# Issuing one head pair's values and the next pair's scores as one step of the attention that runs beside the feed-forward

## The chip, the cores and the metric

One core of one Trainium2 chip runs the whole kernel. The metric is device time in microseconds (us). A kernel is run several times and the median is given; one further execution was recorded by the hardware profiler, and all views shown here come from it.

## The reference

Four batches of 768 tokens go through two blocks, all in float32. The first is attention with 8 heads of 64: each token sees the tokens nearer than 16 places and 24 block summaries (maximum of the keys, mean of the values, over blocks of 32 tokens). The second takes the heads side by side as x of 768 x 512, adds the real part of a two-dimensional Fourier transform, normalises, and adds a feed-forward with 2048 hidden units.

```python
k_sum = k.reshape(B, H, nb, block, D).max(axis=3)
v_sum = v.reshape(B, H, nb, block, D).mean(axis=3)
scores_l = scale * q @ k.T                  # masked to |i - j| < 16
scores_s = scale * q @ k_sum.T + log(32)
a = softmax(concat([scores_l, scores_s]))   # over both together
x = a @ concat([v, v_sum])                  # heads side by side: (4, 768, 512)
u = x + real(fft(fft(x, axis=1), axis=2))
un = (u - mean(u)) / sqrt(var(u) + 1e-6)
out = u + relu(un @ w_ch1) @ w_ch2          # 512 -> 2048 -> 512
```

## The kernel before

The instructions are written in Python as generators. A scheduler puts them into each engine's queue by program order as priority, moving an instruction that it expects to be ready ahead of one that it does not; once written, each queue runs in that order.

**Stages.** The attention of batch 0 comes first, in an order fixed by hand (`first_attention`). Then, for each batch b: the Fourier stage and normalisation (`gen_fourier`, lines 1043 to 1160), and the feed-forward in two halves, `gen_hidden(b, 0)`, `gen_out(b, 0)`, `gen_hidden(b, 1)`, `gen_out(b, 1)`. Products use a seven-product scheme for 2 x 2 blocks, so `gen_hidden` has four j of seven products each and yields four times per j: 16 steps; `gen_out` of a first half has 12 steps. The chain `most` of hidden, out, hidden is thus 44 steps. The second out half runs together with the next batch's Fourier stage. During batch 0 the weights are also converted from 64-bit to 32-bit floats (`gen_weights`), by VectorE (DVE) and ScalarE (ACT), and stored for the later batches.

**Attention of batches 1 to 3.** `gen_attention(b)` (line 884) runs beside the previous batch's stages. A batch has four head pairs g. For each pair:

- `prepare` (line 676): 12 transposes on TensorE (PE) into four PSUM tiles `qk`, eight ACT copies into `kt` and `qt` (line 698), and a DVE maximum over the key blocks, `km` (line 700). It is issued one pair ahead.
- `scores` (line 751): 48 small matrix products of the near keys into two PSUM tiles `sc` (line 759), an exponential on ACT for each (line 765) and a DVE multiplication of each by the mask `near`.
- `sum_scores` (line 769): four products with the block maxima into the tile `ss` (line 775) and an exponential on ACT (line 776).
- `values` (line 778): one product for the block means into the PSUM tile `vs` (line 782), a DVE multiplication into the SBUF tile of the same name, 48 small products into two PSUM tiles `av` (line 792), six more that add the block means (line 797), then for each `av` a DVE reciprocal (line 801) and a DVE multiplication into x.

The profile counts two PE records for each of these products. `load` and `load_values` issue the DMAs of q, k and v for later pairs on the SP queue, on which the feed-forward's weights are fetched too.

**PSUM.** The eight banks are two pools of four: `abank` (tag `attn`) for every attention tile above and for the Fourier stage of later batches, `bank` for the feed-forward (tiles X, Y, Z).

**A hidden j in four steps.** Step 1: product into X, ACT copies X to c11 (line 1187); product into Y, DVE adds it. Step 2: product into X, ACT copies X to c12 (line 1192); product into Z, ACT copies it to c22 (line 1194). Step 3: product into X, DVE adds X to c22; product into Z, DVE adds. Step 4: product into X, ACT writes c21 (line 1203); the rest is DVE. X accumulates over four products, so each product into X waits until the reading of the one before has ended.

**Mixing.** `drive` takes its generators in proportion. Counting the steps of `most`, the 12 attention steps of a batch come after

```
scores                  4  15  26  37
sum_scores + prepare    8  19  30  41
values + load_values   11  22  33  44
```

for the attention of batches 2 and 3. For batch 1 six steps fall into the Fourier stage of batch 0 (the first of them a prepare of its own), and the other seven go one to four steps of `most`, beside twelve steps of weights.

Of the kernel before, what the change touches and what calls it, by code (L numbers as in the profile page):

```python
# [489 lines left out]
def _main_program(ctx, tc, q, k, v, moe_w_ch1, moe_w_ch2, out):  # L490
# [3 lines left out]
    B, H, S, D = q.shape  # L494
# [5 lines left out]
    NP = H // 2  # L500
# [54 lines left out]
    def abank(shape, name):  # L555
        return psum.tile(shape, FP, tag="attn", bufs=4, name=name)
# [6 lines left out]
    def tt(out, in0, in1, op):  # L563
        nc.vector.tensor_tensor(out=out, in0=in0, in1=in1, op=op)  # L564
# [7 lines left out]
    def load(b, g, *which):  # L572

        for n in which or (1, 0):
            t = nat[b, g, n] = apool.tile([P, 2, NST // 2, 2 * D], FP, tag="nat", bufs=4, name=f"{'qk'[n]}n_{b}_{g}")
            fetch(out=t.rearrange("p e j n -> p (e j) n"),
                  in_=(q, k)[n][b, 2 * g:2 * g + 2].rearrange("e (j p s) d -> p (e j) (s d)", p=P, s=2))
# [61 lines left out]
    def load_values(b, g):  # L639
        if is_wide(b):  # L640
            load_wide_values(b, g)
            return
        if g % 2 and following(b, g, 1) and (b, g) != (1, 1):
            block_sums(*divmod((b * NP + g + 1) // 2, NP // 2))
        load_narrow_values(b, g)

    def load_wide_values(b, g):

        vw, off = wide_vw(g), v[b, 2 * g].offset
        for r0, r1, i0, i1 in ((0, WK, 1, NQ - 1), (W, WK, 0, 1), (0, WK - W, NQ - 1, NQ)):  # L650
            for e in range(2):
                fetch(out=vw[r0:r1, e, i0:i1, 0:D],
                      in_=bass.AP(v.tensor, off + (S * e + QB * i0 - W + r0) * D,
                                  [[D, r1 - r0], [QB * D, i1 - i0], [1, D]]))
# [96 lines left out]
    def scores(b, g):  # L751
        kt, qt = kt_bufs[g % 2], nat[b, g]
        ps = [abank([P, NB2, BLOCK], f"sc_{b}_{g}_{h}") for h in range(2)]
        for i in range(NB2):
            for h in range(2):
                o = BLOCK * (NB2 * h + i)
                for e in range(2):
                    rows, r = slice(D * e, D * (e + 1)), 64 * (e ^ h)
                    nc.tensor.matmul(ps[h][r:r + 64, i, :], kt[rows, o:o + 64], qt[rows, o:o + BLOCK],  # L759
                                     start=True, stop=True)  # L760
        p = apool.tile([P, 2, NQ, QB], FP, tag="p", name=f"p_{b}_{g}")
        pm = p[:, 1].rearrange("p n c -> p (n c)")[:, 0:S2]
        p = p[:, 0].rearrange("p (h i) (j c) -> p h (i j) c", h=2, c=BLOCK)
        for h in range(2):
            nc.scalar.activation(out=p[:, h], in_=ps[h], func=AF.Exp, scale=SC)
            tt(p[:, h], p[:, h], near[:, h], ALU.mult)
        return p, pm

    def sum_scores(b, g, p):
        km, qt = km_bufs[g % 2], nat[b, g]  # L770
        ps = abank([P, S2], f"ss_{b}_{g}")
        for h in range(2):
            for e in range(2):
                rows, r = slice(D * e, D * (e + 1)), 64 * (e ^ h) + 32 * h
                nc.tensor.matmul(ps[r:r + 32, :], km[rows, :], qt[rows, S2 * h:S2 * (h + 1)], start=True, stop=True)
        nc.scalar.activation(out=p, in_=ps, func=AF.Exp, scale=SC)

    def values(b, g, p, pm, x):
        vw = vw_bufs[g % 2]
        ps = abank([P, D], f"vs_{b}_{g}")  # L780
        vb, pick = sums[b, g]
        nc.tensor.matmul(ps, pick, vb, start=True, stop=True)
        tt(vs[:, :, 0:D], ps[:, None, :].to_broadcast([P, 2, D]),
           half_of[:, :, None].to_broadcast([P, 2, D]), ALU.mult)

        av = [abank([P, NST, D1], f"av_{b}_{g}_{r}") for r in range(2)]
        for t in range(NST):
            h = t // HT
            for j in range(4):
                for r in range(2):  # L790
                    rows, i = slice(64 * r, 64 * (r + 1)), 4 * t + j
                    nc.tensor.matmul(av[r][32 * j:32 * (j + 1), t, :], p[rows, h, i - NB2 * h, :], vw[rows, i, :],
                                     start=(t == 0), stop=False, skip_group_check=True)
        for t in range(HT):
            for r in range(2):
                rows = slice(64 * r, 64 * (r + 1))
                nc.tensor.matmul(av[r][:, t:t + HT + 1:HT, :], pm[rows, P * t:P * (t + 1)], vs[rows],
                                 start=False, stop=(t == HT - 1), skip_group_check=True)
        for r in range(2):
            rc = rec[:, b * NP + g, r]  # L800
            nc.vector.reciprocal(out=rc, in_=av[r][:, :, D])
            xo = x[:, 0, P * g + D * r:P * g + D * (r + 1)]
            xo = bass.AP(xo.tensor, xo.offset, [list(xo.ap[0]), [HT * DM + D * (1 - 2 * r), 2], [DM, HT], [1, D]])
            tt(xo, av[r].rearrange("p (h t) d -> p h t d", h=2)[:, :, :, 0:D],
               rc.rearrange("p (h t) -> p h t", h=2)[:, :, :, None].to_broadcast([P, 2, HT, D]), ALU.mult)
# [3 lines left out]
    def following(b, g, n):  # L809
        i = b * NP + g + n  # L810
        return divmod(i, NP) if i < B * NP else None
# [72 lines left out]
    def gen_attention(b):  # L884
        x = bpool.tile([P, NST, DM], FP, tag="x", bufs=2, name=f"x_{b}")
        x_of[b] = x
        for g in range(NP):
            p, pm = scores(b, g)
            yield
            sum_scores(b, g, pm)  # L890
            n1, n2, n3 = (following(b, g, n) for n in (1, 2, 3))
            if n1:
                prepare(*n1)
            if n3:
                load(*n3)
            yield
            values(b, g, p, pm, x)
            if n2:
                load_values(*n2)
            yield  # L900


# [402 lines left out]
    def drive(*gens):  # L1305


        gens = list(gens)
        rounds = max(g[1] for g in gens)
        while gens:  # L1310
            for s in range(rounds):
                for g in list(gens):
                    gen, n, ahead = g
                    for _ in range(n * (s + 1) // rounds - n * s // rounds):
                        with tc.high_priority(ahead) if ahead else ExitStack():
                            done = next(gen, gens) is gens
                        if done:
                            gens.remove(g)
                            break

    def first(gen, n):
        for _, step in zip(range(n), gen):
            yield

    weights = gen_weights()
# [15 lines left out]
        yield from gen_attention(1)  # L1341

    attn = second_attention()
    drive((gen_fourier(0), 4, 600), (first(weights, 66), 12, 0), (first(attn, 6), 1, 0))
    block_sums(1, 1)
    for b in range(B):


        most = chain(gen_hidden(b, 0), gen_out(b, 0), gen_hidden(b, 1))
        if b == 0:  # L1350
            in_order[0] = False
            drive((most, 4, 0), (weights, 12, 0), (attn, 1, 0))
            done_weights.append(True)
        else:
            drive((most, 11, 0), (gen_attention(b + 1) if b + 1 < B else iter(()), 3, 0))
        last = gen_out(b, 1)
        if b + 1 < B:
            drive((gen_fourier(b + 1), 22, 600), (last, 12, 0))
        else:
            drive((last, 1, 0))  # L1360
        if b == B - 2:

            ok = apool.tile([P, B * NP * 2 * NST], FP, tag="qt", name="ok")
            all_ok = spool.tile([P, 2], FP, tag="all_ok", name="all_ok")
            flag = cpool.tile([1, 1], I32, name="flag")
            rv = rec.rearrange("p n h i -> p (n h i)")
            nc.vector.tensor_scalar(out=ok, in0=rv, scalar1=1.0 / LIM, scalar2=None, op0=ALU.is_ge)
            nc.vector.scalar_tensor_tensor(out=ok, in0=rv, scalar=LIM, in1=ok, op0=ALU.is_le, op1=ALU.mult)
            nc.vector.tensor_reduce(out=all_ok[:, 0:1], in_=ok, op=ALU.min, axis=AX.X)
            nc.vector.memset(all_ok[:, 1:2], 1.0)  # L1370
            ps = bank([1, 1], "flag_ps")
            nc.tensor.matmul(ps, all_ok[:, 0:1], all_ok[:, 1:2], start=True, stop=True)
            nc.vector.tensor_scalar(out=flag, in0=ps, scalar1=P - 0.5, scalar2=None, op0=ALU.is_lt)
# [40 lines left out]
```

## Time and profile before

| | |
|---|---|
| median of 3 runs | 826.65 us (822.34 to 828.26) |
| the profiled execution | 829.18 us, of which 827.4 us is the span of the instructions |
| PE, share of the span | 97% |
| DVE, ACT, POOL | 59%, 31%, 2% |
| DMA | 120.53 MB, mean 146 GB/s |

Busy time is how long an engine had an instruction in it; for PE the ends of matrix products are modelled and overlap, so the starts are the better measure. In a timeline row the columns are the start and the length in us, the engine, the line, the operation with the tile it writes and those it reads, their shapes, and how many instructions are merged in the row; a bracket gives idle time of the engine before it and what ended that. "PEld" is the loading of PE's stationary operand.

### The profile page before, as it was taken

To read this page: it belongs to the slowest core of one execution; us is meant where nothing else is said; L and a number is where in the kernel's file an instruction comes from. 1 tells how busy PE (TensorE), PEld (TensorE's weight loads), DVE (VectorE), ACT (ScalarE), POOL (GpSimd) and SP (SyncE) were. 2 spreads that over 40 slices of the span, in tenths; PEclk is the share of its full clock that TensorE was granted. 3 is DMA by queue.
4 is the path that set the end of the run, shared out by engine and by line. 5 is a ranking of instruction groups with operands and counts; after the bars stand their busy time and mean duration, and the time that the engine had idled before them with its cause. 6 is when DMAs were issued, how large, how long until landed. Compare 5 with 4: busy or idle time off the path is not lost.

```text
span 827.4 us, 14641 instructions
## 1 busy us (share of the span) xinstructions
PE 798.8 (97%) x6038; PEld 583.6 (71%) x6038; DVE 486.9 (59%) x1117; ACT 254.6 (31%) x561; POOL 20.0 (2%) x31
## 2 busy tenths in 40 slices
PE   9979998999999999999999999999999999999997
PEld 6767655445589855786669875787669875786686
DVE  5769997987998643533367823542348933532351
ACT  3534756453635023203234313121323501101200
POOL 0010000000000200020000000000000000000000
PEclk9969999999999999999999999999999999999999
DMA  9997797969633276246453253423312234205001
GB/s 217 222 240 153 195 257 230 291 220 306 228 129 115 72 279 185 87 94 217 112 121 99 87 210 122 128 39 122 131 46 90 71 131 188 90 0 223 0 27 54
DMA packets 101611, 120.53 MB, mean 146 GB/s; under 512 B 50560, under 2 KB 83552, under 8 KB 101344
## 3 DMA queue, kind: packets, MB, share of 16 engines
q1 hardware_dynamic: 100848, 119.31, 49.2%
q8 instruction: 49, 0.80, 0.4%
q10 hardware_dynamic: 688, 0.20, 0.1%
q14 instruction: 26, 0.21, 0.1%
HBM read 96.96 MB, written 22.54 MB: 144 GB/s over the span
## 4 chain that ended last, share of the span: by engine, by line
PE 81%; DVE 10%; ACT 5%; DMA 2%; issue 1%; POOL 0%; SPq 0%; DVEq 0%; ACTq 0%; POOLq 0%
PE hx L1177 18%; PE ox L1241 16%; PE hz L1177 9%; PE oz L1241 8%; PE o L1218 4%; PE y L1077 4%; PE hy L1177 4%; PE oy L1241 4%; PE sc L759 2%; PE mx L1036 2%; DVE x L564 1%; DVE w L564 1%; ACT qt L698 1%; PE y L1081 1%; PE qk L696 1%
## 5 line engine op out<-in xcount | busy, mean ns | idle before, releaser
L1177 PE MATMUL hx<-u,w 128*128 128x384 f32 x512 | 186.7, 492 | 7.8 <-DVE h L564 3.9
L1177 PEld LDWEIGHTS hx<-u,w 128*128 128x128 f32 x512 | 94.9, 191 | 72.9 <-DVE h L564 7.3
L1177 PE MATMUL hz<-u,w 128*128 128x384 f32 x256 | 94.6, 493 | 0.0
L1241 PE MATMUL ox<-w,s 128*128 128x256 f32 x336 | 81.2, 381 | 0.4 <-DVE x L564 0.3
L1241 PE MATMUL oz<-w,s 128*128 128x256 f32 x336 | 80.7, 379 | 0.0
L1241 PE MATMUL ox<-w,h 128*128 128x256 f32 x336 | 78.3, 381 | 0.3 <-DVE x L564 0.3
L1177 PEld LDWEIGHTS hz<-u,w 128*128 128x128 f32 x256 | 49.0, 192 | 34.6 <-ACT h L1194 1.0
L564 DVE TENSOR_TENSOR x<-ox,x 128x256 f32<-128x256 f32 x84 | 35.4, 423 | 61.5 <-PE ox L1241 61.2
L1241 PEld LDWEIGHTS ox<-w,h 128*128 128x128 f32 x336 | 63.3, 190 | 10.9 <-DVE x L564 1.4
L1241 PEld LDWEIGHTS ox<-w,s 128*128 128x128 f32 x336 | 62.7, 190 | 9.3 <-DVE x L564 1.2
L1241 PEld LDWEIGHTS oz<-w,s 128*128 128x128 f32 x336 | 63.4, 190 | 8.2
L564 DVE TENSOR_TENSOR h<-hx,h 128x384 f32<-128x384 f32 x32 | 17.8, 556 | 67.8 <-PE hx L1177 67.0
L1187 ACT COPY h<-hx 128x384 f32<-128x384 f32 x32 | 15.3, 477 | 127.7 <-PE hx L1177 116.0
L564 DVE TENSOR_TENSOR h<-hy,h 128x384 f32<-128x384 f32 x32 | 17.8, 557 | 60.7 <-PE hy L1177 57.5
L1177 PE MATMUL hy<-u,w 128*128 128x384 f32 x128 | 46.6, 487 | 0.0
L1218 PE MATMUL o<-w,h 128*128 128x512 f32 x96 | 42.6, 596 | 1.2 <-DVE w L564 1.2
L1203 ACT ACTIVATE h<-hx 128x384 f32<-128x384 f32 x32 | 15.7, 489 | 79.3 <-PE hx L1177 79.3
L1241 PE MATMUL oy<-w,h 128*128 128x256 f32 x168 | 39.9, 379 | 0.0
L1077 PE MATMUL y<-fs,fold 128*128 128x193 f32 x192 | 37.2, 340 | 0.2
L1177 PEld LDWEIGHTS hy<-u,w 128*128 128x128 f32 x128 | 24.2, 190 | 17.0 <-DVE w L564 0.6
L564 DVE TENSOR_TENSOR x<-oz,x 128x256 f32<-128x256 f32 x42 | 17.8, 423 | 29.5 <-PE oz L1241 29.5
L1241 PEld LDWEIGHTS oy<-w,h 128*128 128x128 f32 x168 | 32.0, 190 | 4.3
(142 smaller groups left out, 1096.8 us busy)
## 6 DMA issues: line engine op xcount, KB each, us to landing
w<-dw SPq DMA_DIRECT2D x44, 896.0 KB, 5.6
words<-in_moe_w_ch_dram SPq DMA_DIRECT2D x32, 512.0 KB, 6.2
dw<-w SPq DMA_DIRECT2D x12, 896.0 KB, 7.1
vw<-in_v_dram SPq DMA_DIRECT2D x47, 192.0 KB, 5.2
kn<-in_k_dram SPq DMA_DIRECT2D x16, 384.0 KB, 4.7
qn<-in_q_dram SPq DMA_DIRECT2D x16, 384.0 KB, 5.9
out_dram<-x SPq DMA_DIRECT2D x24, 256.0 KB, 2.0
fs<-c_fs SPq DMA_DIRECT2D x8, 579.0 KB, 3.6
```

Of the source, the lines that this page charges most:

```text
L564: nc.vector.tensor_tensor(out=out, in0=in0, in1=in1, op=op)
L696: nc.tensor.transpose(ps[:, P * j:P * (j + 1)], src[:, e, j, :], ident)
L698: nc.scalar.copy(out=dst[D * e:D * (e + 1), s:S:2], in_=ps[D * s:D * (s + 1)])
L759: nc.tensor.matmul(ps[h][r:r + 64, i, :], kt[rows, o:o + 64], qt[rows, o:o + BLOCK], start=True, stop=True)
L1036: nc.tensor.matmul(out, y[:, g], table, start=False, stop=True, skip_group_check=True)
L1077: nc.tensor.matmul(y, fgs[par][:, st, P * g:P * (g + 1)], fs[par][:, g % 2, st, :], start=(st == 0), stop=(st == HT - 1))
L1081: nc.tensor.matmul(y, zq[:, par, s2], fs[par][:, 0, s2, :], start=False, stop=False, skip_group_check=True)
L1177: nc.tensor.matmul(ps, w[:, a, kk, :], u[:, r, kk, :], start=start and kk == 0, stop=stop and kk == 1, skip_group_check=True)
L1187: nc.scalar.copy(out=c11, in_=X)
L1203: nc.scalar.activation(out=c21, in_=X, func=AF.Relu)
L1218: nc.tensor.matmul(ps, h[:, n, hf, P * t:P * (t + 1)], wt[2, b, j][:, 2 * hf:2 * hf + 2, :], start=(n, hf) == (0, 0), stop=(n, hf) == (NC ...
L1241: nc.tensor.matmul(ps, left[a][:, n, :], wt[2, b, j][:, r, :], start=start and n == 0, stop=stop and n == NC - 1, skip_group_check=True)
```

## The change

A pair's `values` is issued at the start of the step in which the next pair's `scores` and `sum_scores` are issued; `load_values` follows them in that step. `prepare` and `load` have a step to themselves. The loop runs once more for the last pair's values, so a batch has nine steps in place of twelve. Nothing is computed differently, and the number of instructions stays.

The mixing follows: in the Fourier stage of batch 0 five steps in place of six, then one to five of `most` with fifteen of weights, and for batches 2 and 3 nine steps spread over all 44 of `most`.

```diff
     def gen_attention(b):
         x = bpool.tile([P, NST, DM], FP, tag="x", bufs=2, name=f"x_{b}")
         x_of[b] = x
-        for g in range(NP):
-            p, pm = scores(b, g)
-            yield
-            sum_scores(b, g, pm)
-            n1, n2, n3 = (following(b, g, n) for n in (1, 2, 3))
+        held = None
+        for g in range(NP + 1):
+            if held:
+                values(b, g - 1, *held, x)
+            if g < NP:
+                held = scores(b, g)
+                sum_scores(b, g, held[1])
+            if g and (n1 := following(b, g, 1)):
+                load_values(*n1)
+            yield
+            if g == NP:
+                return
+            n1, n3 = (following(b, g, n) for n in (1, 3))
             if n1:
                 prepare(*n1)
             if n3:
                 load(*n3)
-            yield
-            values(b, g, p, pm, x)
-            if n2:
-                load_values(*n2)
             yield
...
-    drive((gen_fourier(0), 4, 600), (first(weights, 66), 12, 0), (first(attn, 6), 1, 0))
+    drive((gen_fourier(0), 4, 600), (first(weights, 66), 12, 0), (first(attn, 5), 1, 0))
...
-            drive((most, 4, 0), (weights, 12, 0), (attn, 1, 0))
+            drive((most, 5, 0), (weights, 15, 0), (attn, 1, 0))
...
-            drive((most, 11, 0), (gen_attention(b + 1) if b + 1 < B else iter(()), 3, 0))
+            drive((most, 44, 0), (gen_attention(b + 1) if b + 1 < B else iter(()), 9, 0))
```

## The prediction

> **What bounds the kernel now.** I read the page's busy times first, then busy time by stage, then PE's timeline, then all engines around the few gaps in it.
>
> ```profile
> span 827.4 us, 14641 instructions
> PE 798.8 (97%) x6038; PEld 583.6 (71%) x6038; DVE 486.9 (59%) x1117; ACT 254.6 (31%) x561; POOL 20.0 (2%) x31
> ```
>
> ```profile
> 76.00:101.00 25.00, 22.58 (x389) 16.15 (x389) 24.45 (x71) 19.37 (x37) 0.00 (x0) 0.93 0.66 150
> 101.00:146.00 45.00, 41.06 (x416) 24.96 (x414) 40.32 (x83) 26.23 (x53) 0.00 (x0) 0.96 0.85 256
> ...
> 484.67:618.86 134.19, 133.04 (x1285) 92.36 (x1283) 51.86 (x114) 32.75 (x68) 0.74 (x1) 1.00 0.39 122
> 675.36:786.00 110.64, 110.64 (x404) 76.16 (x403) 39.83 (x85) 15.39 (x32) 0.00 (x0) 1.00 0.30 113
> ```
>
> After the length of each stretch come PE, PEld, DVE, ACT and POOL with counts, PE's clock, DMA share and GB/s. Two regimes are to be seen. While weights are converted (76 to 146 us) DVE is the fuller engine and PE has gaps. Later PE is full and DVE under 40%: the third row is the feed-forward of batch 2 with the attention of batch 3, the fourth about the same stretch of batch 3 with none. Only what PE spends counts there, so I looked at how attention sits in PE's queue:
>
> ```profile
> 492.41 1.45 PE L1177 MATMUL hx<-u,w 128*128 128x384 f32 x4
> 493.79 1.60 PE L759 MATMUL sc<-qt,kt 64*64 64x32 f32 x96
> 495.33 1.56 PE L1177 MATMUL hx<-u,w 128*128 128x384 f32 x4
> 496.72 1.45 PE L1177 MATMUL hy<-u,w 128*128 128x384 f32 x4
> ...
> 503.17 1.45 PE L1177 MATMUL hx<-u,w 128*128 128x384 f32 x4
> 504.55 0.85 PE L775 MATMUL ss<-qt,km 64*32 64x384 f32 x8
> 505.33 0.88 PE L696 MATMUL qk<-ident,kn 128*128 128x128 f32 x6
> ...
> 517.22 0.94 PE L797 MATMUL av<-vs,p 64*128 64x130 f32 x12
> 518.10 2.85 PE L1177 MATMUL hx<-u,w 128*128 128x384 f32 x8
> 520.78 1.46 PE L1177 MATMUL hy<-u,w 128*128 128x384 f32 x4
> ```
>
> Start to start, an undisturbed dense product takes 1.29 us. Ahead of `sc` it is 1.38 and after it 1.39; ahead of `ss` 1.38; after `values` two products take 2.68, not 2.58. Each entry to or exit from small tiles costs 0.09 to 0.10 us. Last, a gap in this stage:
>
> ```profile
> 505.92 2.05 ACT L698 COPY kt<-qk 64x384 f32<-64x384 f32 x4
> 507.99 2.02 ACT L698 COPY qt<-qk 64x384 f32<-64x384 f32 x4
> 510.04 0.48 ACT L1187 COPY h<-hx 128x384 f32<-128x384 f32 x1
> 510.57 1.56 PE L1177 MATMUL hx<-u,w 128*128 128x384 f32 x4 [1.12 <-ACT h L1187]
> ```
>
> The eight copies of a `prepare` fill ACT for four microseconds; the c11 copy of a hidden j queues behind them and PE stops 1.12 us.
>
> [...] The kernel gives attention four, and early on the trace shows them run short: PE and DVE rows of batch 1's attention.
>
> ```profile
> 101.28 0.33 PE L782 MATMUL vs<-vbs,sel 96*128 96x64 f32 x2
> 114.51 0.29 DVE L564 TENSOR_TENSOR vs<-vs,half 128x128 f32<-128x128 f32 x1
> 115.78 0.94 PE L797 MATMUL av<-vs,p 64*128 64x130 f32 x12
> ...
> 110.05 1.59 PE L759 MATMUL sc<-qt,kt 64*64 64x32 f32 x48 [0.58 <-ACT p L765]
> ```
>
> DVE reaches the multiplication of `vs` 13 us after its product, so `vs` and both `av` stay occupied; the scores have one bank, and the second half waits for the exponential of the first.
>
> **The change part by part.** Instructions stay, so PE's own work stays. Counting `drive`'s proportions (a step falls at the next whole step of `most` after 44k/9), the merged steps come at 5, 15, 25, 35 and 44, `prepare` at 10, 20, 30 and 40.
>
> 1. Tile switches, batches 2 and 3. A pair now pays 0.19 around `sc`; 0.14 around `ss` (0.09 in, 0.05 out, the first transposes taking 0.71 us where the next six take 0.66); 0.10 after `values`, whose entry through the full-width `vs` is free. That is 0.43 a pair, 1.72 a batch. After: the first step has scores alone, 0.19; three have values, scores, sums, with a free entry, 0.10 at the exit, and one unknown switch s from the values' 64 x 128 tiles to the scores' 64 x 64; the last 0.10. From `sc` to `ss` nothing is added: at 76.02 us, where they already follow each other, `ss` starts 1.53 us after `sc`, as long as `sc` takes when alone. A `prepare` alone enters free (at 123.39 us its first six take 0.66). Sum 0.59 + 3s. Nothing shown has that switch; s lies between 0 and 0.10, and a gain is excluded since the products remain. I take 0.05 [...]. Saved 1.72 - 0.74 = 0.98 a batch, 1.96 for two (1.7 to 2.3).
>
> 2. The place of `prepare`. From starts against 1.29 per product, a `prepare` costs 1.38 at step 8 (before a j's first step: c11 late), 1.49 at 41 (after the first: c12 late), 0.31 at 30 (after the second: only the DVE addition to c22 is late, held by `km`), nothing at 19, in the out stage, which leaves ACT idle. The new places 10 and 30 are of the kind of 30, 20 of 19, and 40, after a fourth step, of 8. The batch driven beside batch 1 has all four: before 1.38 + 0.31 + 1.49 = 3.18, after 0.31 + 0.31 + 1.38 = 2.00. Beside batch 2 the last is missing: 1.69 becomes 0.62. Saved 1.18 + 1.07 = 2.25. That the exponential of `ss` leaves this step gains nothing, since the first copy waits about as long for its transposes.
>
> 3. The merged step needs six PSUM tiles from four banks. `sc` takes the free bank and that of `vs`; `ss` needs an `av` bank. With DVE under 40% busy this is covered: at step 22 the multiplication of `vs` ends 0.56 us after its product starts, while the `av` products take two microseconds; the first `av` is read 0.9 us after they end, under the 1.54 us of `sc`. Without that cover it costs up to about 1 us a step. PE issues no dense product for 4.6 us, so the dense readings catch up; three exponentials (0.49 each) and two masks (0.51 each) follow at its end, where the next dense reading has over 1 us of slack. Zero.
>
> 4. DMAs. `load_values` stays behind the release of its buffer by the same `values`, now also after `scores` and `sum_scores` in program order, which use no DMA; weights queued behind it on SP wait as before. `load` stays with `prepare`. A landing takes 5 to 6 us against 25 us or more until use. Zero.
>
> 5. Batch 1, beside weight conversion. The merges save perhaps 0.4. But scores, masks and `km` are issued one to nine steps earlier, ahead of conversion in DVE's order, and DVE has little room. PE's waits here are 2.3 us for a DVE addition at 128.76 and 1.2 for converted weights at 154.33. Two masks go ahead of the latter: +1.0. A `km` (0.95) may go ahead of the former: +0.5. Bounds: half of the 7.6 us of gaps between 76 and 196 us (PE busy 112.4 of 120) vanish (-3.8), or bank shortage repeats at each merged step (+8 to +11, below). I take +1.1.
>
> Sum: -1.96 - 2.25 + 1.1 = -3.1. The profiled execution's 829.18 (span 827.4 and 1.8 around it) would be 826.1. It stands 2.5 above the median; from the median, 823.5.
>
> **The rivals.**
> A. The scheduler doesn't keep the merged step together: it puts `ss` or `sc` between later dense products. It did so at 105 to 112 us, and at 90 us two dense products lie between. Against: in batches 2 and 3 each group stands whole. Then the switches return (+1.96) and the places stay: -1.2, 825.5.
> B, slower. The bank shortage of the early stage, from the merged order. Scores 16 and 20 steps of `most` in were apart from values; now values 2 and scores 3 are issued at once, at step 15, as values 1 and scores 2 at step 5. If DVE is late again by 13 us or more and the scheduler expects it earlier, PE stands in front of a bank with dense work behind it. It decides from the point where DVE reaches `vs` later than PE exhausts what stands ahead of the scores. Price: two such steps at 4 to 5 us (three waits of the 0.6 seen, plus most of a 2.3 us gap) and items 1 and 2 lost in part: +9 to +12, 836 to 839. For: 13 us late, DVE at 90 to 98%. Against: PE's gaps there are hidden in part, as DVE sets that stage's end.
> C, faster. The early stage gains: with fewer entries PE's and DVE's orders fit better and half of the gaps go: -4.2 - 0.4 - 3.8 = -8.4, 818.3.
>
> **How the numbers follow.** Chances: forecast 0.48, A 0.18, B 0.23, C 0.11. About 1%, or 8.3 us, is what a measurement of this kernel can tell from no change. A lies within it, B is beyond, C on its edge. Of the forecast a little falls outside. So faster 0.10, within 0.66, slower 0.24. The likeliest case alone spans 819.5 to 828. The range reaches into C and to the middle of B: 817.5 to 837.
>
> **What would show it.** Right: in the stretches of batches 1 and 2, `vs`, `av`, `sc`, `ss` in one run of about 4.6 us, one 0.10 after it; the stretch 484.67 to 618.86 shorter by about 2.05 of its 134.19 us; no 1.1 us gap before c11 at the first `prepare`, one left beside batch 1 at the last; 76 to 196 us longer by about one. Wrong: a bracketed wait ahead of `sc` or `ss` for a DVE `vs` or x; small groups split by dense products; gaps at 10 or 30 of the size of step 8's; or the early stage moving by more than 4 us.

## The result and the profile after

The kernel after takes 824.57 us (median of 22 runs, 819.49 to 827.17), the kernel before on the same chip 828.36 us (22 runs): the ratio is 0.995, with a 95% interval of 0.9931 to 0.997. The forecast was 823.5 us, and 3.1 us less than before; 3.8 us less was measured. The total was met by luck, not by the steps that led to it: the feed-forward stages were to give 4.2 us and gave less than one, and the early stage was to cost 1.1 us and gave two to three.

The profiled execution took 823.95 us. Its page:

```profile
span 822.2 us, 14639 instructions
PE 795.1 (97%) x6038; PEld 583.2 (71%) x6038; DVE 484.5 (59%) x1117; ACT 254.5 (31%) x561; POOL 19.7 (2%) x31
```

Of the 5.2 us that this span is shorter, 3.3 lie before the first scores of batch 1 (72.70 us after, 76.02 before). PE's queue has the same order there in both kernels, and in the profiles of all the kernels below that point lies between 71.96 and 76.68 us, with merged and with unmerged steps at either end. It goes with the granted clock (0.95 against 0.91 up to there; PE is busy 64.25 us against 67.23 with the same 750 records) and is not the change's. The timed runs show the same scatter: in 163 runs of the kernel before, 0.01 of mean granted clock goes with 5.5 us. So stages are compared from the first scores of batch 1 on. Busy time by stage of before, then of after: early stage, feed-forward of batch 1 with the attention of batch 2, feed-forward of batch 2 with the attention of batch 3. The first figure after the stretch is its length, the second PE's busy time; clock, DMA share and GB/s end the row.

```profile
76.02:195.94 119.92, 112.34 (x1136) 64.88 (x1135) 109.86 (x246) 66.92 (x125) 0.00 (x0) 0.97 0.82 234
288.99:427.81 138.82, 134.82 (x1298) 93.45 (x1296) 57.84 (x131) 36.69 (x76) 6.92 (x8) 1.00 0.53 158
484.67:618.86 134.19, 133.04 (x1285) 92.36 (x1283) 51.86 (x114) 32.75 (x68) 0.74 (x1) 1.00 0.39 122
```

```profile
72.70:191.79 119.09, 113.53 (x1136) 66.03 (x1136) 107.74 (x244) 65.70 (x122) 0.00 (x0) 0.97 0.89 241
284.58:423.67 139.09, 134.26 (x1297) 94.06 (x1296) 57.59 (x131) 36.40 (x76) 6.58 (x8) 1.00 0.52 158
480.79:614.27 133.48, 132.16 (x1285) 93.06 (x1283) 51.68 (x114) 32.60 (x68) 0.74 (x1) 1.00 0.39 123
```

The early stage leaves PE idle 5.6 us in place of 7.6; it is only 0.8 us shorter, as PE is busy 1.2 us longer with as many records, and what takes that time was not found. Beside batch 1 the stage is 0.27 us longer (forecast: 2.16 shorter), beside batch 2 it is 0.71 shorter (forecast: 2.05). What a merged step looks like, in PE's timeline of after, beside batch 2; the columns are those of the rows above, with idle time in brackets:

```profile
519.78 0.33 PE L782 MATMUL vs<-vbs,sel 96*128 96x64 f32 x2
520.04 1.20 PE L792 MATMUL av<-vw,p 64*32 64x65 f32 x96
521.17 0.94 PE L797 MATMUL av<-vs,p 64*128 64x130 f32 x12
522.04 1.60 PE L759 MATMUL sc<-qt,kt 64*64 64x32 f32 x96
523.90 0.85 PE L775 MATMUL ss<-qt,km 64*32 64x384 f32 x8 [0.26 <-DVE x L564]
524.68 1.56 PE L1181 MATMUL hx<-u,w 128*128 128x384 f32 x4
```

The group stands whole. From the last `av` products to `sc` pass 0.87 us, no more than to the dense product that followed them before (0.88): the unknown switch s costs nothing. But `ss` stands 0.26 us until the first `av` is read and its bank is free. The next merged step of the same stage:

```profile
555.01 0.33 PE L782 MATMUL vs<-vbs,sel 96*128 96x64 f32 x2
555.27 1.20 PE L792 MATMUL av<-vw,p 64*32 64x65 f32 x96
556.41 0.94 PE L797 MATMUL av<-vs,p 64*128 64x130 f32 x12
557.28 1.13 PE L759 MATMUL sc<-qt,kt 64*64 64x32 f32 x62
559.34 0.77 PE L759 MATMUL sc<-qt,kt 64*64 64x32 f32 x34 [0.94 <-issue]
```

Within one group of the same operands PE stops 0.94 us, for nothing that the profile shows. The same happens beside batch 1:

```profile
395.71 1.35 PE L759 MATMUL sc<-qt,kt 64*64 64x32 f32 x74
397.92 0.55 PE L759 MATMUL sc<-qt,kt 64*64 64x32 f32 x22 [0.86 <-issue]
```

And beside batch 1 a wait for DVE is new; DVE's and PE's rows of after there, then DVE's of before at the same place:

```profile
305.73 0.42 DVE L564 TENSOR_TENSOR w<-w 128x256 f32<-128x256 f32 x1 [4.79 <-DMA w<-dw]
306.07 0.55 DVE L564 TENSOR_TENSOR h<-hx,h 128x384 f32<-128x384 f32 x1
...
306.68 2.85 PE L1181 MATMUL hx<-u,w 128*128 128x384 f32 x8 [1.19 <-DVE h L564]
```

```profile
308.36 0.56 DVE L564 TENSOR_TENSOR h<-hx,h 128x384 f32<-128x384 f32 x1 [2.92 <-PE hx L1177]
309.29 0.42 DVE L564 TENSOR_TENSOR w<-w 128x256 f32<-128x256 f32 x1 [0.38 <-DMA w<-dw]
```

Before, the dense addition came first on DVE and the sum of weights, which waits for a DMA, after it. Now the sum stands ahead of the addition, and PE behind both. Some 13 us earlier, at the start of the stage, PE waits for DVE in either kernel. The rows of before, of after, and of after with 64 tiny products at its very start (a run described below):

```profile
298.52 1.56 PE L1177 MATMUL hx<-u,w 128*128 128x384 f32 x4 [1.63 <-DVE h L564]
...
293.68 2.85 PE L1181 MATMUL hx<-u,w 128*128 128x384 f32 x8 [1.20 <-DVE h L564]
...
296.04 4.54 PE L1181 MATMUL hx<-u,w 128*128 128x384 f32 x8 [2.26 <-DVE h L564]
```

The third kernel has the order of after on DVE and PE, but all its wait is in the first place and none in the second. So the two waits have to be taken together, and each alone scatters between profiles of one order. The accounts of the two stages, start to start:

| us | beside batch 1 | beside batch 2 |
|---|---|---|
| tile switches, as forecast but with s = 0 | -1.13 | -1.13 |
| place of `prepare`, as forecast | -1.18 | -1.07 |
| `ss` waits for a bank | +0.32 | +0.32 |
| gap inside `sc` | +1.14 | +1.21 |
| DVE: new wait at 306.68; the stage's first wait 1.20, was 1.63 | +1.45 - 0.43 | |
| sum | +0.17 | -0.67 |
| measured | +0.27 | -0.71 |

The first two rows are the forecast's, not measured in these two profiles, so a sum that comes out within 0.1 us is a check of the account and no proof of each row.

### The profile page after: what moved, and what is told of

It is laid out like the page before. It is cut to its first block, busy times and chain, and to the rows that moved or that the text cites. A ratio compares the mean times of both kernels' runs of the same rounds, so it can differ in the third digit from the quotient of the medians.

```text
span 822.2 us, 14639 instructions
## 1 busy us (share of the span) xinstructions
PE 795.1 (97%) x6038; PEld 583.2 (71%) x6038; DVE 484.5 (59%) x1117; ACT 254.5 (31%) x561; POOL 19.7 (2%) x31
## 4 chain that ended last, share of the span: by engine, by line
PE 74%; DVE 16%; ACT 4%; DMA 3%; issue 2%; SPq 0%; POOL 0%; DVEq 0%; ACTq 0%; POOLq 0%
PE ox L1245 16%; PE hx L1181 15%; PE oz L1245 8%; PE hz L1181 7%; PE o L1222 4%; PE y L1081 4%; PE hy L1181 4%; PE oy L1245 4%; DVE w L564 3%; DMA w<-dw 2%; DVE x L564 2%; PE mx L1040 2%; DVE h L564 2%; ACT kt L698 1%; PE sc L759 1%
## 5 line engine op out<-in xcount | busy, mean ns | idle before, releaser
L1081 PE MATMUL y<-fs,fold 128*128 128x193 f32 x192 | 35.3, 329 | 0.3 <-DMA fm<-c_fm 0.3
```

What stands on the lines that cost most here:

```text
L1081: nc.tensor.matmul(y, fgs[par][:, st, P * g:P * (g + 1)], fs[par][:, g % 2, st, :], start=(st == 0), stop=(st == HT - 1))
```

## The experiments

**Parts alone.** Theory: the gain is the early stage's and that of the place of `prepare`; merging in the feed-forward stages earns its switches and pays them back. Four kernels take the change apart.

Merged steps for batches 2 and 3 only; batch 1 as before:

```diff
-        yield from gen_attention(1)
+        yield from gen_three(1)              # the three steps of before
...
-            drive((most, 11, 0), (gen_attention(b + 1) if b + 1 < B else iter(()), 3, 0))
+            drive((most, 44, 0), (gen_merged(b + 1) if b + 1 < B else iter(()), 9, 0))
```

> The merged steps and the 9 in 44 only for the attention of batches 2 and 3; batch 1 as before. Theory 1 (each stretch pays by its own PE queue): the change's stretches beside batches 1 and 2 already sum to about +0.3 and -0.7 us in the two profiles, so -0.4 to -1 us in all, ratio about 0.999. Theory 2 (the measured -3.8 us is the saved switches and the new places of prepare, as predicted): -3 to -4 us, ratio 0.996. Batch 1's stage, to about 290 us, as long as before's.

Measured: 826.96 us (22 runs), ratio 0.9991 (0.997 to 1.0012): 0.7 us less, and by the interval between 2.5 less and 1.0 more.

Merged steps for batch 1 only, with its mixing (5 of `most` to 15 of weights); batches 2 and 3 as before:

```diff
-        yield from gen_attention(1)
+        yield from gen_merged(1)
...
-    drive((gen_fourier(0), 4, 600), (first(weights, 66), 12, 0), (first(attn, 6), 1, 0))
+    drive((gen_fourier(0), 4, 600), (first(weights, 66), 12, 0), (first(attn, 5), 1, 0))
...
-            drive((most, 4, 0), (weights, 12, 0), (attn, 1, 0))
+            drive((most, 5, 0), (weights, 15, 0), (attn, 1, 0))
```

> The merged steps only for batch 1's attention, beside weight conversion; batches 2 and 3 with twelve steps as before. Theory 1: most of the -3.8 us comes from here, -1 us from the order between 76 and 289 us, and what a less throttled start adds; ratio 0.996 to 0.998. Theory 2: the prediction's +1.1 us, ratio 1.001.

Measured: 825.04 us (22 runs), ratio 0.9959 (0.9941 to 0.9976). That is 3.4 us, but not all of it need be the early stage's order. The mean granted clock of these runs was 0.9911, against 0.9895 for before, which by the slope above goes with 0.9 us. And in its profile PE's idle time in the early stage is 1.1 us less than before, while 1.6 us are gained between the first hidden products of batch 1 and of batch 3, where PE's order is that of before.

Only the places: three steps a pair as before, for batches 2 and 3 after chosen steps of `most`, so that scores and values move too (`drive_at` lets the attention take a step after each listed one).

```diff
-            drive((most, 11, 0), (gen_attention(b + 1) if b + 1 < B else iter(()), 3, 0))
+            drive_at(most, gen_attention(b + 1) if b + 1 < B else iter(()),
+                     (5, 10, 13, 15, 20, 23, 25, 30, 33, 35, 40, 44))
```

> The three steps of a pair as before, batch 1 as before; for batches 2 and 3 sum_scores with prepare come at steps 10, 20, 30, 40 of most, scores at 5, 15, 25, 35, values at 13, 23, 33, 44. Theory of the prediction: the wait of a prepare goes with its place in j; the stretch beside batch 1 loses 1.1 us, that beside batch 2 1.4 us, no change of switches: -2.4 us, ratio 0.997. Rival: where prepare stands does not matter, and a stall of about 1.4 us follows it anywhere: ratio 1.000.

Measured: 825.91 us (12 runs), ratio 0.9966 (0.9947 to 0.9984).

Only the merging: batches 2 and 3 in merged steps, with `prepare` at the old 8, 19, 30 and 41 (merged steps at 4, 15, 26, 37 and 44), batch 1 as before.

> The merged steps for batches 2 and 3 at about the old places: prepare at 8, 19, 30, 41, the others at 4, 15, 26, 37, 44; batch 1 as before. Theory of the prediction: 1.1 us of switches saved per stretch, stalls behind prepare as before (about 1.4 at 8 and 41): -2.2 us, ratio 0.997. Rival (the merged step pays for itself): the six merged steps have gaps of 0.3 us before ss or 1.1 us within sc in two to four of them, so -1 to +2 us, ratio 0.999 to 1.003.

Measured: 828.87 us (22 runs), ratio 1.0013 (0.9994 to 1.0033). PE's timeline of it, beside batch 2:

```profile
511.49 1.56 PE L1200 MATMUL hx<-u,w 128*128 128x384 f32 x4 [1.17 <-ACT h L1210]
529.90 0.85 PE L775 MATMUL ss<-qt,km 64*32 64x384 f32 x8 [0.26 <-DVE x L564]
568.35 1.01 PE L759 MATMUL sc<-qt,kt 64*64 64x32 f32 x53 [0.73 <-issue]
```

The c11 copy is late again (511.49), as the old place of `prepare` makes it, and the two waits of the merged step are there with it. What follows from the four: the two halves add up to the change (0.9959 x 0.9991 = 0.995); the places alone are worth 2.8 us by their ratio, about the 2.25 of item 2 (in the profile 1.50 us beside batch 1, 0.42 of it in the stage's first wait, and 1.09 beside batch 2, from one batch's first hidden product to the next one's); merging alone is worth nothing in the late stages. There the interval leaves room for half a microsecond of gain, not for the 1.96 of item 1.

**What the gap inside `sc` is.** Numbering all of PE's records in the trace of after (products, weight loads and the waits of its sequencer), the gaps at 397.92 and 559.34 us come before records 6850 and 9410: 194 + 26 x 256 and 194 + 36 x 256. One queue of instructions moved 49 packets of 16,384 bytes, and PE has 12,227 records, 47.8 times 256; from the start of its first packet to that of its 48th, 254 of PE's records start per packet. From these numbers it is estimated that the queue brings PE's instructions, in blocks of 256; the runs below test that.

```profile
q8 instruction: 49, 0.80, 0.4%
```

The DMA records show a packet of this queue from 395.29 to 396.46 us and one from 556.50 to 557.71; PE goes on 1.5 and 1.6 us after they end. By that count the block before had begun at 394.23 and 555.70, so PE is in the next block 3.69 and 3.64 us later; a merged step uses some 428 instructions in 4.6 us, so 256 of them would last 2.8 us. To test this, the queue was moved against its blocks: 32 products of one column at the very start are 128 instructions more (64 products and 64 weight loads by the trace's count), and no order changes.

```diff
+    for i in range(32):
+        nc.tensor.matmul(ps[0:1, 0:1], zeros[:, 0:1], zeros[:, 0:1], start=True, stop=True)
     nc.scalar.dma_start(out=wide, in_=dr["wide"].ap())
```

> The kernel after with 32 matrix products of one column more at the very start, which moves all later PE instructions by 128 places in PE's instruction stream and changes no order. Theory (instruction fetch): the gaps of 0.86 and 0.94 us inside sc, which end for nothing that the profile shows, lie where 256 PE instructions have been used up faster than the next 256 come. So they leave the merged step at 35 beside batch 1 and the one at 25 beside batch 2, and come up where a multiple of 256 now falls 99 or 151 instructions into the step: step 35 beside batch 2 and step 25 beside batch 1, perhaps also step 15 beside batch 1 (67). Each costs about 1.2 us; with two or three of them the time is that of after within 1.5 us (0.994 to 0.997 of before). Rival (something else at that place holds sc, such as a PSUM bank or a copy of kt that the profile doesn't name): both gaps stay at 35 beside batch 1 and 25 beside batch 2, and no other step gets one.

Measured: 837.38 us (6 runs), ratio 1.0107 (1.0065 to 1.0149). The gaps in PE's timeline:

```profile
136.25 0.84 PE L759 MATMUL sc<-qt,kt 64*64 64x32 f32 x14 [3.60 <-issue]
...
344.39 0.89 PE L759 MATMUL sc<-qt,kt 64*64 64x32 f32 x45 [0.97 <-issue]
380.35 0.55 PE L759 MATMUL sc<-qt,kt 64*64 64x32 f32 x22 [0.41 <-issue]
604.93 0.77 PE L759 MATMUL sc<-qt,kt 64*64 64x32 f32 x35 [0.36 <-issue]
```

Both old gaps are gone, and the new ones are in the steps named: 15 and 25 beside batch 1, 35 beside batch 2. The forecast of the time missed by far. It left out the early stage: at 136.25 us PE stands 3.6 us at a block's end, and at 108.53 us, a block's end again, 1.89 us for an ACT conversion by the profile's account. The block before the first began at 130.31 us, its packet was moved only from 133.76 to 134.76, and PE went on 1.5 us later. With the DMA engines 80% busy in that stage the packet starts 3.5 us after the block, at the later gaps shown here 0.7 to 1.1. Why it starts late there was not tried. These two stops are 5.5 us, and this kernel is 12.8 us above after at the medians. Part of the rest goes with the granted clock: it is 0.50 from 109.1 to 115.9 us and from 136.5 to 143.2 us, just behind the two stops, and the mean of the six timed runs is 0.982 against 0.989 for before, some 4 us by the slope above. That a stop brings on the lower clock is not shown; behind the gaps at 397.92 and 559.34 us of after the clock stays at 1.00.

Two controls followed: after with 64 such products (256 instructions, so that each block begins where it did), and before with 32.

> The kernel after with 64 products of one column at its start: PE's later instructions move by 256 places, a whole block of 16 KiB, so that every block begins at the same instruction as in after. Theory (instruction fetch): the two gaps inside sc are back where after has them, in the step at 35 beside batch 1 and in that at 25 beside batch 2, at 0.7 to 1.2 us; no gap of several us in the early stage; time as after, 0.993 to 0.997 of before, whatever the 64 products cost at the start (under 2 us, beside the first transfers). Rival (it is the products at the start themselves, not the place of the blocks, that made the kernel with 32 of them slower): slower still, 1.01 or more.

Measured: 825.93 us (20 runs), ratio 0.9969 (0.9952 to 0.9987), at the upper end of what was expected.

```profile
400.38 0.55 PE L759 MATMUL sc<-qt,kt 64*64 64x32 f32 x22 [0.72 <-issue]
...
561.68 0.76 PE L759 MATMUL sc<-qt,kt 64*64 64x32 f32 x34 [0.79 <-issue]
```

Both gaps are back at the same product, with the same 22 and 34 records behind them. So it is not the products at the start that cost, but where the blocks end.

> The kernel before with the same 32 products of one column at its start, in the same order otherwise. Theory (only the merged step, some 428 PE instructions in 4.6 us, outruns the fetch): no unexplained gap over 0.3 us beside batches 1 and 2, and none of several us early; time within 2 us of before, 0.998 to 1.003. Rival (the early stage outruns the fetch in either order, and before only happens to lie well): a gap for nothing that the profile shows of 1 us or more between 76 and 196 us, 1.003 or more; then part of what the merged batch 1 gains may be luck of the same kind.

Measured: 828.45 us (20 runs), ratio 1.0013 (0.9996 to 1.003), and no gap over 0.3 us without a named cause in either stage. In the two positions of its blocks that were run, the order with small groups between dense products shows no such stop. In the merged kernels it depends on where in the step, of some 430 records, a block ends. Where that is 53 to 115 records into the step, PE stopped at the next block's end, 256 records on, each time (11 steps, 0.36 to 0.97 us); where it is at up to 42 or from 170 on, never (19 steps). These are the 30 merged steps with scores of batches 2 and 3 in the five profiles whose steps are built alike: after, the two parts with late merging, and after with 32 and with 64 products ahead.

**Six tiles from four banks.** The product for `vs` and its multiplication were moved into the step of `prepare`, to leave the merged step more banks.

```diff
             if n3:
                 load(*n3)
+            mean_values(b, g)     # the vs product and its multiplication, no longer in values
             yield
```

> The kernel after with the product of the block means and its multiplication on DVE moved from the merged step into the prepare step before it, so that only two av tiles and the three of the scores are needed at once. Theory (ss waits for the bank of an av because the merged step wants six tiles from four banks): the 0.26 us waits of ss for x at step 15 go, and the values no longer wait for vs in the early stage (1.8 and 0.7 us); in exchange vs holds a bank longer, and prepare's four qk tiles may wait for one. Span 0.5 to 2.5 us below that of after (822.2). Rival (the bank that vs now holds from prepare to values is missing to the four qk tiles): a new wait of PE ahead of a qk of 0.5 us or more in each prepare, about 12 of them, span 3 to 6 us above.

One run: 823.85 us, span 822.1. The main expectation was wrong: without `vs` the step still wants two `av`, two `sc` and `ss`, five from four.

```profile
328.59 0.85 PE L775 MATMUL ss<-qt,km 64*32 64x384 f32 x8 [0.35 <-DVE x L564]
...
523.22 0.85 PE L775 MATMUL ss<-qt,km 64*32 64x384 f32 x8 [0.35 <-DVE x L564]
```

The wait grew from 0.26 to 0.35 us, and six `vs` products now wait for a copy of `prepare`, 1.3 us in all. The 0.66 us that the values wait for `vs` at 178.80 us in after did go. The span equals that of after (822.2), but a single run can't tell a microsecond.

**Versions without the new waits.** If the merged step pays for its length, one dense step in its middle should keep the gain. Values are issued one step of `most` ahead of the next pair's scores and sums, and the last `prepare` comes at 38, after a j's second step like that at 30, in place of 40. The diff is against after; `gen_split` is a copy of `gen_attention` with this edit.

```diff
             if held:
                 values(b, g - 1, *held, x)
+                if (n1 := following(b, g, 1)):
+                    load_values(*n1)
+                yield
             if g < NP:
                 held = scores(b, g)
                 sum_scores(b, g, held[1])
-            if g and (n1 := following(b, g, 1)):
-                load_values(*n1)
...
-            drive((most, 44, 0), (gen_attention(b + 1) if b + 1 < B else iter(()), 9, 0))
+            drive_at(most, gen_split(b + 1) if b + 1 < B else iter(()),
+                     (5, 10, 15, 16, 20, 25, 26, 30, 34, 35, 38, 44))
```

> The kernel after, but beside batches 1 and 2 the values of a pair are issued one step of the feed-forward ahead of the next pair's scores and sums (at 15, 25, 34 for values, 16, 26, 35 for scores and sums; the last values at 44), and the last prepare at 38 in place of 40. Theory (the merged step pays for its saved switches with a shortage of PSUM banks and of PE instructions): no wait of ss for x and no unexplained gap inside sc, at 0.1 to 0.2 us for one entry more per pair (six in all, about +1); the waits that go are 0.3 x 2 and 1.2 x 2, and the 1.46 us of the prepare at 40 becomes about 0.3, so about 3 us less than after: 0.990 to 0.993 of before. Rival (those waits are only moved, since PE, DVE and ACT have the same work in the same stretch): within 1 us of after, 0.994 to 0.997.

Measured: 822.12 us (7 runs), ratio 0.9923 (0.9893 to 0.9953). PE's timeline at the step that had waited for the bank:

```profile
521.13 0.94 PE L797 MATMUL av<-vs,p 64*128 64x130 f32 x12
522.00 1.56 PE L1204 MATMUL hx<-u,w 128*128 128x384 f32 x4
523.49 1.60 PE L759 MATMUL sc<-qt,kt 64*64 64x32 f32 x96
525.02 0.85 PE L775 MATMUL ss<-qt,km 64*32 64x384 f32 x8
```

No gap inside `sc`, no wait of `ss`, and none for a `prepare`. In its profile 194.27 us lie between the first hidden product of batch 1 and that of batch 2 (after: 196.21), and 189.37 between that and the one of batch 3 (after: 190.31): 2.9 us less, the three that were expected. The two waits for DVE at the start of the stage beside batch 1 stay, at 1.35 and 1.34 us.

The other way to combine was merged steps in batch 1 and three steps at chosen places in batches 2 and 3.

> Merged steps for batch 1 only, and three steps a pair for batches 2 and 3 at chosen places (prepare at 10, 20, 30, 40; scores at 5, 15, 25, 35; values at 13, 23, 33, 44). Theory (the early part and the place of prepare bring the gain, and both add): 0.9959 x 0.9966 = 0.9925 of before, about 822 us, and beside batches 1 and 2 no unexplained gap inside sc. Rival (the two gains are one and the same, the DVE waits at the start of the feed-forward beside batch 1, which both kernels lost): 0.9955 or more, no better than the early part alone.

Measured: 824.65 us (22 runs), ratio 0.9953 (0.9933 to 0.9974). The product of the parts would have been 0.9925, below this interval; but the parts' own intervals leave that product between about 0.990 and 0.995, so the timings don't exclude that they add. In the profile of the merged batch 1 alone the first wait for DVE beside batch 1 was 0.30 us; here it is 1.72:

```profile
293.52 2.85 PE L1200 MATMUL hx<-u,w 128*128 128x384 f32 x8 [1.72 <-DVE h L564]
```

That is 1.4 of about 2 us missing. Whether the combination causes it is not shown: before, the same with 32 products ahead, and the merged batch 1 alone have one order of PE and DVE there, and their first wait is 1.63, 1.37 and 0.30 us. The single profiles of the parts scatter by as much as what is missing.

Last, the split order in the late batches alone, with batch 1 as before, beside the split version once more:

> The kernel before for batch 1, and for batches 2 and 3 the order with values one step of the feed-forward ahead of scores and sums and the last prepare at 38. Theory (the late part loses its gain only to the waits that the merged step makes; without them the prediction's items 1 and 2 come in): saved against before are the switches, 1.72 less about 0.9 a batch, and nearly all of the prepares' cost, so about 4 us less from 289 us on in the profile, and 0.9955 to 0.9975 of before; merged alone gave 0.9991 there. Rival (the feed-forward beside batches 1 and 2 has a floor set elsewhere, by DVE or by the weights): no better than merged alone, 0.998 or more.

Measured: 824.69 us (22 runs), ratio 0.9956 (0.9935 to 0.9977).

> The same kernel as split38, once more beside the kernel with that order in the late batches alone. Theory: 0.991 to 0.994 of before, and lower than split_late by what the merged batch 1 alone gave (0.4%). Rival (the early gain is the luck of where PE's blocks of instructions begin, which the late order shifts for nothing that comes earlier): the two differ by less than 0.2%.

Measured: 822.22 us (9 runs), ratio 0.993 (0.9905 to 0.9954). The late part without the merged step's waits is worth 3.6 us by its ratio, where merging it whole gave 0.7; the merged batch 1 adds about 2.5 to that at the medians. The two intervals overlap, so these runs alone don't decide against the rival that was named. The split version is 2.4 us below the kernel after at the medians of all their runs and is the best of the kernels here, though its intervals against before overlap that of after.

## Why the prediction was right in its sum and wrong in its steps

1. **Tile switches.** Right in kind and nearly in size: no switch from `values` to `scores` (s = 0 where 0.05 was taken), so 1.13 a batch in place of 0.98. But that gain was paid back in the merged step itself (item 3).
2. **The place of `prepare`.** Right. The gap before c11 at the first `prepare` is gone and the last one beside batch 1 has its 1.20 us wait, as the forecast named. The places alone measured 2.8 us (1.3 to 4.4) for 2.25, with scores and values moved as well.
3. **Six tiles from four banks: "Zero".** Wrong, and this is the step that failed in the late stages. The bank was late by 0.26 us once in each, well inside the bound of one microsecond a step; the argument that the first `av` is read within the 1.54 us of `sc` forgot that DVE may be in other work when `av` ends. Beside batch 2 it is in additions into `s` from 521.04 us on and reads the first `av` from 522.98; in the step at 361.72 us, where nothing waits, it is idle and reads it at 364.08, 0.10 us after `sc` starts. The larger cost was not among the bounds at all: that "PE issues no dense product for 4.6 us" was read as slack for the readers of dense tiles, and not as 428 instructions in 4.6 us, whose next block, in the two steps where PE stopped, was there only 3.6 to 3.7 us after the one before had begun. 1.14 and 1.21 us were measured for it, and a block's end in the early stage cost up to 3.6 us in another position of the blocks.
4. **DMAs: zero.** For the attention's own loads nothing speaks against it. A sum of weights that waits for its DMA came ahead of a dense addition in DVE's order, and that cost 1.45 us less 0.43 beside batch 1. The forecast followed SP's queue and not DVE's. Those two figures are of one profile each. Taken together, the two waits at the start of that stage are 0.3 to 1.7 us in the five profiles with three steps a pair in the late batches, and 1.8 to 3.2 in the nine with merged or split steps, so a cost of this kind is there in all of these; what in the scheduler's choice turns it was not tried.
5. **Batch 1: +1.1.** Wrong in sign. Two waits of before (2.30 us for a DVE addition, 1.22 for converted weights) are not in after; rows of before, then of after:

```profile
128.76 1.64 PE L1177 MATMUL hx<-u,w 128*128 128x384 f32 x4 [2.30 <-DVE h L564]
...
154.33 6.25 PE L1218 MATMUL o<-w,h 128*128 128x512 f32 x14 [1.22 <-DVE w L564]
```

```profile
124.58 1.59 PE L759 MATMUL sc<-qt,kt 64*64 64x32 f32 x48 [0.65 <-ACT p L765]
...
128.58 1.44 PE L1181 MATMUL hx<-u,w 128*128 128x384 f32 x2 [0.73 <-issue]
...
178.80 0.94 PE L797 MATMUL av<-vs,p 64*128 64x130 f32 x12 [0.66 <-DVE vs L564]
```

What is left there is the bank shortage of rival B, at 0.65 us rather than its four to five a step, a block's end at 128.58, and a late `vs` at 178.80. The block's end is a cost of the merged steps here too: of the four other kernels with merged steps in batch 1 and no products ahead, three show such a stop there, of 0.54 to 1.27 us. PE's idle time from the first scores of batch 1 to the second hidden half of batch 0 tells the early part without the clock: 7.4 to 7.8 us in the six kernels with batch 1 in three steps, 4.5 to 6.5 in seven profiles of merged ones, 9.3 in the one with 32 products ahead, 5.5 us of which are its two block ends. So the early stage is worth about two microseconds in PE's idle time, against the three of the timed part. The forecast took DVE for the fuller engine up to 146 us, which its first row shows (24.45 us against PE's 22.58) and its second does not (40.32 against 41.06). It let masks and `km` go ahead of conversion on DVE and priced that delay; it didn't price that the dense additions and conversions no longer stand behind them later. That is argued from the two waits that went; no run shows which DVE instruction set them free.

Of the rivals, A did not happen in batches 2 and 3: the groups stand whole. B had its mechanism and not its price. C's size for the early stage, 3.8 us, was closest to the 3.4 of the timed part, though a quarter of PE's gaps went and not half, together with a late stage worse than any case allowed for. So the number was met by two errors of three to four microseconds with opposite signs, which is luck.

## What to carry to other kernels

A run of many small products is also a rate of instructions: here 256 of them would have taken 2.8 us, PE was in the next block only after 3.6 to 3.7 us and stood for 0.86 and 0.94 us at its start, and 128 instructions more at the kernel's start moved the place. Here a dense product between two such groups was worth more than the last tile switch that merging them saved (0.9956 of before in the late batches with it, 0.9991 without). A wait that one profile shows should be looked for in a second profile of the same order before it is called an effect of a change. And test the parts of a change one by one even if its sum came out as forecast.

## What the runs showed of the hardware that was not expected

Where PE's blocks of instructions end has an effect larger than the change: 128 instructions more at the start took the kernel from 0.995 to 1.011 of before, 256 more to 0.997, and 128 more took the kernel before from 1 to 1.001. Part of the first figure goes with a lower granted clock (a mean of 0.982 against 0.989). At the gaps at 397.92, 559.34 and 128.58 us of after, which end for nothing the profile shows, PE went on 1.5 to 1.6 us after the packet of instructions had landed. Going from 64 x 128 to 64 x 64 and to 64 x 32 tiles cost nothing (0.87 and 1.53 us start to start, as long as the products themselves), while a change between these and dense 128 x 128 products cost 0.09 to 0.10 us each (1.38 and 1.39 us start to start around `sc` in before, against 1.29). So the cost that the forecast counted for a switch is seen here at changes to and from the dense products, and not between the three small tiles.
